# Loads, global keys and output products rescheduled in a fused attention and feed-forward kernel

## The chip, the cores and the metric

The kernel runs on one core of a Trainium2 chip. The metric is the device time of one execution in microseconds (us). Several executions are taken of each kernel, and the kernel before is run on the same chip in the same rounds. Medians and ranges are of all runs; where a slow run moves a median, the median of the fast runs stands beside it.

## The reference, cut to what matters

Attention with four batches, eight heads, 768 positions and 64 features; a query sees the first 8 keys (the global keys) and the last 96. A SwiGLU feed-forward block follows, on the 3072 tokens that come out.

```python
scores = scale * np.matmul(q, k.transpose(0, 1, 3, 2))
is_global = pos[None, :] < 8
is_local = (rel >= 0) & (rel < 96)
dist = np.where(is_global & ~is_local, 96.0, np.abs(rel))
scores = np.where(is_global | is_local, scores - slopes * dist, -1e9)
a = softmax(scores)                     # written out in the reference
x = (a @ v).transpose(0, 2, 1, 3).reshape(3072, 512)
g = x @ w_gate                          # 512 -> 1536
out = (g * sigmoid(g) * (x @ w_val)) @ w_out
```

## The kernel before

TensorE works on fp16 operands. The feed-forward part goes in eight tiles of 384 tokens, each with twelve groups of hidden features: a gate product (`gps`), a value product (`vps`), then the sum-times-gate product (`sl`) and the hidden row (`hT`) on VectorE. The output product of a tile is cut into parts of three matmuls, which are spread over the next tile. The attention of batch (block) b feeds tiles 2b and 2b+1, and its steps are put between the feature groups of the tiles before.

Keys go in seven chunks of 120. A chunk fills 128 rows: eight global rows, then 120 keys of its own. Block 0 is done in two halves of 384 queries, so that the feed-forward part can start early. Chunk 3 holds keys 360 to 479. Half 0 ends at query 383, so of chunk 3 its queries see only the first 24 keys:

```python
SCORES = {(0, 0): [(0, 0, 0, 216), (1, 216, 120, 216)],
          (0, 1): [(2, 0, 240, 144), (3, 144, 360, 24)],   # (chunk, column, first query, queries)
          ...

def load_v_rest(b, c):
    n = min(KC, S - KC * c)                                # KC = 120
    nc.gpsimd.dma_start(
        out=vSs[b][NG:NG + n, c, :, :],                    # NG = 8
        in_=v[b, :, KC * c:KC * c + n, :].rearrange("h p d -> p h d"))
```

The products of weights and values are these. `side is None` gives the denominators, a side gives the numerators:

```python
def weigh(self, half, dst, side):
    parts = self.parts(half)
    for i, (c, cb, col, o, n) in enumerate(parts):
        vals = vSs[b][:, c]
        for j in range(4):
            r = slice(32 * j, 32 * j + 32)
            nc.tensor.matmul(
                dst[r, o:o + n],
                lhsT=ones[:, 0:32] if side is None else vals[:, 4 * g + j, side::2],
                rhs=pairs[b, 2 * g + j // 2].at[cb][:, j % 2, col:col + n],
                start=(i == 0), stop=(i == len(parts) - 1), ...)
```

Heads go in pairs. Block 0 and pairs 0 and 1 of block 1 are transposed by TensorE. Pairs 2 and 3 of block 1 and all of blocks 2 and 3 are loaded as rows (`kst`, `qst`) and transposed by a DMA that SyncE issues. Their eight global rows of each chunk are cleared, and GpSimd copies the global keys in after the transpose:

```python
def stage(b):
    ...
    nc.gpsimd.memset(kend[b], 0.0)
    nc.gpsimd.memset(kst[b][0:NG, 768 * (0 if b > 1 else 2):], 0.0)

def global_keys(self):                                     # of a pair, after its DMA transpose
    k3 = self.kT.rearrange("r (c m) -> r c m", m=128)
    first = k3[:, 0, NG:2 * NG]
    nc.gpsimd.tensor_copy(
        out=k3[:, 0:J, 0:NG], in_=first.unsqueeze(1).broadcast_to([128, J, NG]))
    nc.gpsimd.tensor_copy(out=kE[:, self.hp, 0:NG], in_=first)
```

All loads are issued by GpSimd, in program order. The whole early list is:

```python
for c in range(4):
    load_v_rest(0, c)
...                                  # head: fillers, first transposes
load_w(0, 4); load_w(4, 6)           # gate and value weights of feature groups
load_half(1, 0, H)                   # k and q of block 0, half 1
load_w(6, 8); load_w(8, 10)
for c in range(4, NCH):
    load_v_rest(0, c)
load_w(10, 12)
stage(1); load_qk(1)
for g in range(3):
    load_wo(g)                       # output weights
load_globals()
...                                  # v chunks 0-3, ends, rows of pairs 2 and 3, v chunks 4-6 of block 1
```

The softmax here doesn't subtract the row's maximum and nothing guards it: scores larger than these inputs give would overflow.

## Time and profile before

| what | before |
|---|---|
| median time of the first three runs (range) | 256.95 us (254.27 to 257.81) |
| span of the profiled run, mean granted TensorE clock | 253.7 us, 0.991 |
| TensorE busy | 95% of the span |
| first feature group of tile 0 starts | 16.84 us |
| scores of pair 3 of block 1 start | 68.94 us |
| first gate of tile 2 starts | 78.55 us |

The page gives busy shares by engine and by fortieths of the span. The list of waits tells what ended TensorE's idle time, and the timeline places each of these waits. A timeline row gives the start and the length in us, the engine, the line of the kernel, the operation with output and inputs, the shapes and how many instructions the row merges. A number in brackets at its end is the idle time before the row, with what ended it. The lines are shown in the prediction.

### The profile page before, as it was taken

To read this page: it belongs to the slowest core of one execution; us is meant where nothing else is said; L and a number is where in the kernel's file an instruction comes from. 1 tells how busy PE (TensorE), PEld (TensorE's weight loads), DVE (VectorE), ACT (ScalarE), POOL (GpSimd) and SP (SyncE) were. 2 spreads that over 40 slices of the span, in tenths; PEclk is the share of its full clock that TensorE was granted. 3 is DMA by queue.
4 is the path that set the end of the run, shared out by engine and by line. 5 is a ranking of instruction groups with operands and counts; after the bars stand their busy time and mean duration, and the time that the engine had idled before them with its cause. 6 is when DMAs were issued, how large, how long until landed. Compare 5 with 4: busy or idle time off the path is not lost.

```text
span 253.7 us, 6001 instructions
## 1 busy us (share of the span) xinstructions
PE 240.2 (95%) x2380; PEld 135.3 (53%) x2380; DVE 157.5 (62%) x338; ACT 129.6 (51%) x288; POOL 127.5 (50%) x161
## 2 busy tenths in 40 slices
PE   7998998989799999979999999999999999999994
PEld 4554665545355555544555555555555555555543
DVE  4477766557575666772775666776775567555510
ACT  4746677785453744543563564455734643332321
POOL 8965996392319998918808877813020232300000
PEclk9999999999999999997999999999999999999999
DMA  8999999999911999999933999991011101101122
GB/s 153 164 193 193 171 145 194 177 131 123 145 41 44 89 143 125 170 150 98 110 55 25 125 133 179 151 122 45 0 44 41 41 3 45 41 3 41 41 83 83
DMA packets 93251, 25.76 MB, mean 102 GB/s; under 512 B 81480, under 2 KB 90280, under 8 KB 93224
## 3 DMA queue, kind: packets, MB, share of 16 engines
q0 software_dynamic: 71088, 14.00, 73.4%
q1 hardware_dynamic: 21576, 11.03, 22.6%
q8 instruction: 18, 0.29, 0.5%
q10 hardware_dynamic: 560, 0.36, 0.4%
q14 instruction: 9, 0.07, 0.1%
HBM read 28.58 MB, written 6.29 MB: 137 GB/s over the span
## 4 chain that ended last, share of the span: by engine, by line
PE 73%; DMA 14%; ACT 4%; POOL 3%; DVE 2%; issue 1%; DVEq 0%; POOLq 0%
PE ops L537 22%; PE gps L508 21%; PE vps L508 21%; DMA vS<-in_v_dram 5%; DMA q<-in_q_dram 4%; PE sc L364 3%; DMA qT<-qst 3%; PE num L435 3%; DMA wv<-in_moe_w_val_dram 3%; PE den L435 2%; POOL vS L160 1%; ACT at L372 1%; ACT th L519 1%; PE ops L553 1%; PE sc L328 1%
## 5 line engine op out<-in xcount | busy, mean ns | idle before, releaser
L521 DVE SCALAR_TENSOR_TENSOR sl<-th,gps 128x384 f32<-128x384 f32 x94 | 52.0, 553 | 57.2 <-ACT th L519 56.5
L519 ACT ACTIVATE th<-gps 128x384 f32<-128x384 f32 x94 | 46.6, 496 | 64.3 <-PE gps L508 62.7
L508 PE MATMUL gps<-xT,wg 128*128 128x384 f16 x376 | 77.5, 328 | 1.6 <-DVE xT L470 1.5
L508 PE MATMUL vps<-xT,wv 128*128 128x384 f16 x376 | 77.3, 328 | 1.5 <-DVE sl L521 1.5
L537 PE MATMUL ops<-wo,hT 128*128 128x512 f16 x276 | 73.6, 382 | 0.0
L525 DVE TENSOR_TENSOR hT<-vps,sl 128x384 f16<-128x384 f32 x94 | 51.9, 552 | 9.1 <-PE vps L508 2.2
L508 PEld LDWEIGHTS <-wg 128*128 128x128 f16 x384 | 36.6, 98 | 34.6 <-issue 3.7
L508 PEld LDWEIGHTS <-wv 128*128 128x128 f16 x384 | 36.6, 98 | 27.4 <-issue 3.7
L470 POOL TENSOR_TENSOR xT<-ns,rb 128x384 f16<-128x384 f32 x24 | 24.0, 1017 | 46.4 <-DVE rb L451 45.3
L372 ACT ACTIVATE at<-sc 128x432 f16<-128x432 f32 x72 | 33.3, 534 | 11.5 <-PE sc L364 11.5
L537 PEld LDWEIGHTS <-hT 128*128 128x128 f16 x276 | 26.1, 98 | 24.1 <-issue 1.5
L160 POOL DMA_DIRECT2D vS<-in_v_dram x28 | 24.9, 899 | 1.1 <-issue 1.0
L543 ACT ACTIVATE osb<-ops 128x512 f32<-128x512 f32 x23 | 13.7, 597 | 18.5 <-PE ops L537 18.5
L184 POOL DMA_DIRECT2D kst<-in_k_dram x20 | 17.7, 899 | 4.3 <-DMA wo<-in_moe_w_out_dram 4.3
L466 ACT COPY ns<-num 128x384 f32<-128x384 f32 x28 | 12.0, 482 | 12.7 <-PE num L435 12.7
L184 POOL DMA_DIRECT2D qst<-in_q_dram x20 | 17.2, 879 | 0.1
L383 DVE TENSOR_TENSOR at<-at,masks 128x864 f16<-128x864 f16 x20 | 12.4, 620 | 7.6 <-ACT at L372 7.6
L435 PE MATMUL num<-at,vS 128*32 128x216 f16 (+6 forms) x576 | 12.5, 225 | 2.0 <-DMA vS<-in_v_dram 2.0
L383 POOL TENSOR_TENSOR at<-at,masks 128x864 f16<-128x864 f16 x4 | 7.3, 1818 | 13.3 <-ACT at L372 13.3
L347 ACT ACTIVATE at<-sc 128x432 f16<-128x432 f32 (+2 forms) x32 | 11.6, 455 | 2.6 <-PE sc L339 2.6
L435 PEld LDWEIGHTS <-vS 128*32 128x32 f16 x576 | 10.0, 95 | 2.5 <-DMA vS<-in_v_dram 2.5
L364 PE MATMUL sc<-qT,kT 64*128 64x216 f16 (+2 forms) x148 | 9.7, 249 | 1.4 <-DMA qT<-qst 1.4
(69 smaller groups left out, 175.0 us busy)
## 6 DMA issues: line engine op xcount, KB each, us to landing
out_dram<-osb SPq DMA_DIRECT2D x23, 256.0 KB, 2.8
vS<-in_v_dram POOLq DMA_DIRECT2D x24, 120.0 KB, 6.8
qst<-in_q_dram POOLq DMA_DIRECT2D x20, 96.0 KB, 5.3
kst<-in_k_dram POOLq DMA_DIRECT2D x20, 90.0 KB, 4.3
wo<-in_moe_w_out_dram POOLq DMA_DIRECT2D x3, 512.0 KB, 10.7
wg<-in_moe_w_gate_dram POOLq DMA_DIRECT2D x8, 128.0 KB, 7.8
wv<-in_moe_w_val_dram POOLq DMA_DIRECT2D x8, 128.0 KB, 7.7
wg<-in_moe_w_gate_dram POOLq DMA_DIRECT2D x2, 256.0 KB, 6.6
```

What stands on the lines that cost most here:

```text
L160: nc.gpsimd.dma_start(out=vSs[b][NG:NG + n, c, :, :], in_=v[b, :, KC * c:KC * c + n, :].rearrange("h p d -> p h d"))
L184: nc.gpsimd.dma_start(out=rows_of(st, b, h // 2)[p0:p0 + n, :, h % 2, :], in_=src[b, h, 0:n * J].rearrange("(t p) d -> p t d", p=n))
L364: nc.tensor.matmul(sc[hi][:, col:col + n], lhsT=keys, rhs=self.qT[r, q0:q0 + n], start=True, stop=True)
L372: nc.scalar.activation(out=at[:, hi, :], in_=sc[hi][:, 0:BANK], func=AF.Exp, scale=scale)
L383: mul_eng.tensor_mul(at, at, m[:, :, o:o + BANK])
L435: nc.tensor.matmul(dst[r, o:o + n], lhsT=ones[:, 0:32] if side is None else vals[:, 4 * g + j, side::2], rhs=pairs[b, 2 * g + j // 2].at[c ...
L470: mul_eng.tensor_mul(self.x_out(half, side), srcs[side], self.rb)
L508: nc.tensor.matmul(gv[f, which][:, 0:TB], lhsT=w[:, c, 128 * f:128 * f + 128], rhs=x_of(t)[:, c, :], start=(c == 0), stop=(c == NC - 1))
L519: nc.scalar.activation(out=th, in_=dst[:, 0:TB], func=AF.Tanh, scale=0.5)
L521: nc.vector.scalar_tensor_tensor(out=sl, in0=th, scalar=1.0, in1=dst[:, 0:TB], op0=AluOp.add, op1=AluOp.mult)
L525: nc.vector.tensor_mul(hTs[t][:, f, :], dst[:, 0:TB], gv["sl"])
L537: nc.tensor.matmul(ops, lhsT=hTs[t][:, f, 128 * i:128 * i + 128], rhs=wo[:, f, :], start=(f == 0), stop=(f == NFF - 1))
```

## The change

It is one schedule change with several parts:

- Global keys of all blocks are loaded once (`kG`), and DMAs on SyncE's queue copy them into the rows before the transpose. So the clearing and the copies on GpSimd go.
- Block 1's loads are reordered. The output weights come ahead of the q and k rows, and pair 2 comes ahead of v.
- The last feature group of tile 0 carries four output parts, so these lie between half 1 and block 1. Tile 1 carries two parts in three groups. (In the lists of stretches below, the last two numbers of an entry shift when its attention steps come: work that is kept free of steps at the end, and a head start of the first step.)
- A group's masks (exponentials on ScalarE) are issued after its tanh instead of ahead of it.
- In the head, the first transposes and scores are reordered, there are three more fillers, and one weight load is split.
- The copies of v's global rows are issued two feature groups earlier.
- Of v chunk 3 of block 0, the 24 rows that half 0 needs are loaded early. The other 96 come after the weights of groups 8 and 9.

```diff
 def stage(b):
-        nc.gpsimd.memset(kst[b][0:NG, 768 * (0 if b > 1 else 2):], 0.0)
+        nc.sync.dma_start(out=kend[b][0:NG], in_=kG[:, b])
+        for hp in by_dma(b):
+            pair = kG[:, b, 2 * hp:2 * hp + 2, :].rearrange("p h d -> p (h d)")
+            nc.sync.dma_start(
+                out=rows_of(kst, b, hp)[0:NG].rearrange("p t e d -> p t (e d)"),
+                in_=pair.unsqueeze(1).broadcast_to([NG, J, 2 * D]))
...
-    def load_v_rest(b, c):
-        n = min(KC, S - KC * c)
+    def load_v_rest(b, c, r0=0, r1=KC):
+        r1 = min(r1, S - KC * c)
         nc.gpsimd.dma_start(
-            out=vSs[b][NG:NG + n, c, :, :],
-            in_=v[b, :, KC * c:KC * c + n, :].rearrange("h p d -> p h d"))
+            out=vSs[b][NG + r0:NG + r1, c, :, :],
+            in_=v[b, :, KC * c + r0:KC * c + r1, :].rearrange("h p d -> p h d"))
...  (global_keys and its calls go; load_globals loads kG too)
-    for c in range(4):
+    cut = TB - 3 * KC
+    for c in range(3):
         load_v_rest(0, c)
+    load_v_rest(0, 3, 0, cut)
...  (head: fill(14) -> fill(17), order of transposes and scores)
-    load_w(0, 4)
+    load_w(0, 2)
+    load_w(2, 4)
     load_w(4, 6)
     load_half(1, 0, H)
     load_w(6, 8)
     load_w(8, 10)
+    load_v_rest(0, 3, cut, KC)
     for c in range(4, NCH):
         load_v_rest(0, c)
     load_w(10, 12)
-    stage(1)
-    load_qk(1)
     for g in range(3):
         load_wo(g)
     load_globals()
+    stage(1)
+    load_qk(1)
...  (then ends, pair 2, v chunks 0-3, pair 3, v chunks 4-6)
-        (ff(0, 4, 12), half1, 1.0),
-        (ff(1, 0, 3) + ff(1, 3, 12, (1, 1, 2)), first(1), 6.0),
+        (ff(0, 4, 11) + [(0, 11, 4)], half1, 5.4, 0.4),
+        (ff(1, 0, 12, (0, 1, 1)), first(1), 6.0, -0.1),
...  (masks go to after_gate, run when a group's tanh is issued)
```

More of the change, by code (lines that the diff above doesn't have):

```diff
@@ L156, in load_qk @@
                 out=whole(st, b), in_=src[b, 0:NP].rearrange("h (p j) d -> p h (j d)", p=128))
-    def load_v_rest(b, c):
-        n = min(KC, S - KC * c)
+    def load_v_rest(b, c, r0=0, r1=KC):
+        r1 = min(r1, S - KC * c)
         nc.gpsimd.dma_start(
-            out=vSs[b][NG:NG + n, c, :, :],
-            in_=v[b, :, KC * c:KC * c + n, :].rearrange("h p d -> p h d"))
+            out=vSs[b][NG + r0:NG + r1, c, :, :],
+            in_=v[b, :, KC * c + r0:KC * c + r1, :].rearrange("h p d -> p h d"))
     vG = sb.tile([NG, B, H, D], FP16, name="vG")
+    kG = sb.tile([NG, B, H, D], FP16, name="kG")
     def load_globals():
-        nc.gpsimd.dma_start(
-            out=vG[:, 1:].rearrange("p b h d -> p (b h) d"),
-            in_=v[1:, :, 0:NG, :].rearrange("b h p d -> p (b h) d"))
+        for dst, src in ((kG, k), (vG, v)):
+            nc.gpsimd.dma_start(
+                out=dst[:, 1:].rearrange("p b h d -> p (b h) d"),
+                in_=src[1:, :, 0:NG, :].rearrange("b h p d -> p (b h) d"))
     def copy_globals(b):
@@ L398, in transposes_dma @@
                     in_=rows_of(st, b, hp).rearrange("p t e d -> p (t e d)"))
-        def global_keys(self):
-            k3 = self.kT.rearrange("r (c m) -> r c m", m=128)
-            first = k3[:, 0, NG:2 * NG]
-            nc.gpsimd.tensor_copy(
-                out=k3[:, 0:J, 0:NG], in_=first.unsqueeze(1).broadcast_to([128, J, NG]))
-            nc.gpsimd.tensor_copy(out=kE[:, self.hp, 0:NG], in_=first)
     class Quad:
@@ L586 @@
     V, A = nc.vector.tensor_copy, nc.scalar.copy
-    fill(14)
+    fill(17)
     A(out=q16[:, 0, 0:2], in_=q32)
@@ L609, with load_pair @@
     load_globals()
+    stage(1)
+    load_qk(1)
+    def load_pair(b, hp):
+        for i in (1, 0):
+            for e in range(2):
+                load_rows(b, i, 2 * hp + e)
+    load_ends(1)
+    load_pair(1, 2)
     for c in range(4):
         load_v_rest(1, c)
-    load_ends(1)
-    for hp in by_dma(1):
-        for i in (1, 0):
-            for e in range(2):
-                load_rows(1, i, 2 * hp + e)
+    load_pair(1, 3)
     for c in range(4, NCH):
@@ L619 @@
     p_bias(0, 0, "a0", "a1")
-    sc00 = pairs[0, 0].sc
-    p_bias(0, 1, "a2", "a3")
-    pairs[0, 0].scores_half(0, 0, sc00)
-    p_sc(0, 1)
     p_tr(1, "x2", "o0", V)
+    p_sc(0, 0)
+    p_sc(0, 1, "a2", "a3")
     p_bias(1, 0, "x0", "x1")
-    p_tr(2, "a0", "a1", A)
+    p_tr(2, "a0", "a1", V)
     p_sc(1, 0)
@@ L632 @@
     p_sc(2, 1, "a2", "a3")
+    p_sc(3, 0, "a0", "a1")
     for side, tag in enumerate(("x1", "x2")):
         quads[0, 0].numerators(side, single("num", tag))
-    p_sc(3, 0, "a0", "a1")
     p_sc(3, 1, "a2", "a3")
@@ L682, in fetch @@
         return step
-    def gk(b, *hps):
-        return lambda: [pairs[b, hp].global_keys() for hp in hps]
     def first(b):
         return [[tr(b, 0), tr(b, 1), fetch(b, 2, 3)], [sc(b, 0, 0), sc(b, 0, 1)],
-                [sc(b, 1, 0), sc(b, 1, 1), gk(b, 2)], [va(b, 0, 0), gk(b, 3)],
+                [sc(b, 1, 0), sc(b, 1, 1)], [va(b, 0, 0)],
                 [sc(b, 2, 0), sc(b, 2, 1)], [sc(b, 3, 0), sc(b, 3, 1)], [va(b, 1, 0)]]
@@ L696, in both @@
         return [[sc(b, 0, 2), sc(b, 1, 2)], [sc(b, 2, 2), sc(b, 3, 2), fetch(n, 0, 1)],
-                [va(b, 0, 1)], [va(b, 1, 1), gk(n, 0, 1)],
+                [va(b, 0, 1)], [va(b, 1, 1)],
                 [sc(n, 0, 0), sc(n, 0, 1), fetch(n, 2, 3)], [sc(n, 1, 0), sc(n, 1, 1)],
-                [va(n, 0, 0), gk(n, 2, 3)], [sc(n, 2, 0), sc(n, 2, 1)],
+                [va(n, 0, 0)], [sc(n, 2, 0), sc(n, 2, 1)],
                 [sc(n, 3, 0), sc(n, 3, 1)], [va(n, 1, 0)]]
@@ L710 @@
     stretches = [
-        (ff(0, 0, 4), [], 0),
-        (ff(0, 4, 12), half1, 1.0),
-        (ff(1, 0, 3) + ff(1, 3, 12, (1, 1, 2)), first(1), 6.0),
-        (ff(2, 0, 12, (1,)) + ff(3, 0, 12, (1,)), both(1), 6.0),
-        (ff(4, 0, 12, (1,)) + ff(5, 0, 12, (1,)), both(2), 6.0),
-        (ff(6, 0, 12, (1,)), second(3), 6.0),
-        (ff(7, 0, 12, (1,)), [], 0)]
-    loads = {}
+        (ff(0, 0, 4), [], 0, 0),
+        (ff(0, 4, 11) + [(0, 11, 4)], half1, 5.4, 0.4),
+        (ff(1, 0, 12, (0, 1, 1)), first(1), 6.0, -0.1),
+        (ff(2, 0, 12, (1,)) + ff(3, 0, 12, (1,)), both(1), 6.0, 0.4),
+        (ff(4, 0, 12, (1,)) + ff(5, 0, 12, (1,)), both(2), 6.0, 0.4),
+        (ff(6, 0, 12, (1,)), second(3), 6.0, 0.4),
+        (ff(7, 0, 12, (1,)), [], 0, 0)]
+    loads, after_gate = {}, {}
     def at_step(t, f, *fns):
@@ L724 @@
     for h in range(H):
-        at_step(h // 4, 1 + h % 4, lambda h=h: make_masks(h, WIN, 3 * WIN))
-        at_step(h // 4, (8, 1)[h // 4] + h % 4, lambda h=h: make_masks(h, 0, WIN))
-    at_step(1, 0, lambda: [copy_globals(b) for b in range(1, B)])
+        for (t, f), c0, c1 in zip((((0, h), (0, 8 + h)), ((1, h - 4), (1, h - 2)))[h // 4],
+                                  (WIN, 0), (3 * WIN, WIN)):
+            after_gate.setdefault((t, f), []).append(
+                lambda h=h, c0=c0, c1=c1: make_masks(h, c0, c1))
+    at_step(0, 10, lambda: [copy_globals(b) for b in range(1, B)])
     for b, base, rate, v_at in ((2, 24, 2.0, (30, 31, 32, 32, 37, 38, 39)), (3, 43, 1.4, (54, 55, 56, 57, 61, 62, 63))):
@@ L741 @@
     outs = [(t, i, part) for t in range(NT - 1) for i in range(3) for part in range(4)]
-    for tiles, steps, tail in stretches:
+    for tiles, steps, tail, owed in stretches:
         groups = []
@@ L748 @@
         quota = len(steps) / (work - tail)
-        owed = 0.4
         for w, t, f, which in groups:
@@ L760 @@
                 gate_or_val(t, f, which, NC if t == 0 and f < 2 else 0)
+                for fn in after_gate.pop((t, f), []):
+                    fn()
             owed += w * quota
@@ L767 @@
         assert not steps
-    assert not later and not loads and not outs
+    assert not later and not loads and not after_gate and not outs
     for i in range(2):
```

## The prediction

> **What bounds the kernel now.** I read the page first (busy time and slices), then TensorE's waits, then TensorE's timeline around each wait, then the timelines of GpSimd and SyncE to see what released it.
>
> ```profile
> PE 240.2 (95%) x2380; PEld 135.3 (53%) x2380; DVE 157.5 (62%) x338; ACT 129.6 (51%) x288; POOL 127.5 (50%) x161
> PE   7998998989799999979999999999999999999994
> DMA  8999999999911999999933999991011101101122
> ```
>
> TensorE bounds it: 95% busy, no other engine above 62%. From the nineteenth slice (about 120 us) on, every slice is full until the last; its timeline from 119.6 us has no idle time marked before the closing products. So time can only be won before 120 us, and only what TensorE stands still or runs slow. The DMA engines are full in slices 1 to 11 (to about 70 us) and 14 to 21 (82 to 120 us): in both stretches a transfer cannot come sooner without another coming later.
>
> ```profile
> PE num L435 <- DMA vS<-in_v_dram: 2.0, 3, 1.0
> PE vps L508 <- DVE sl L521: 1.5, 2, 1.0
> PE gps L508 <- DVE xT L470: 1.5, 1, 1.5
> PE sc L364 <- DMA qT<-qst: 1.4, 1, 1.4
> PE den L435 <- DVE at L380: 0.5, 1, 0.5
> ```
>
> Columns: total us, times, longest. These are few and single waits, so each can be placed in the timeline:
>
> ```profile
> 44.87 0.79 PE L508 MATMUL gps<-xT,wg 128*128 128x384 f16 x2 [1.47 <-DVE xT L470]
> 52.24 0.81 PE L508 MATMUL vps<-xT,wv 128*128 128x384 f16 x4 [1.02 <-DVE sl L521]
> 65.76 0.55 PE L364 MATMUL sc<-qT,kT 64*128 64x216 f16 x8 [1.39 <-DMA qT<-qst]
> 114.50 0.25 PE L435 MATMUL num<-at,vS 128*32 128x144 f16 x4 [1.00 <-DMA vS<-in_v_dram]
> 115.97 1.40 PE L508 MATMUL gps<-xT,wg 128*128 128x384 f16 x4
> 119.60 0.81 PE L508 MATMUL gps<-xT,wg 128*128 128x384 f16 x4
> ```
>
> Starts of consecutive gate and value groups stand 0.65 us apart when nothing waits (237.00 after 236.35 us); that is my unit below, and three output products also take 0.65. Measured against it, the standing times are: 1.95 us at 43 to 45.5 (wait and the slow pair after it), 1.2 at 51, 0.6 at 59.6, 1.55 at 64, 0.9 at 72, and 2.5 at 112 to 115. The row at 115.97 takes 1.40 where the same one at 119.60 takes 0.81: the clock was halved after that wait, from 115.97 to 119.6, which costs another 1.55 us. Together 10.3 us, plus about 2 us in the first 26.
>
> GpSimd's timeline shows why the loads come when they do:
>
> ```profile
> 33.62 0.76 POOL L155 DMA_DIRECT2D kst<-in_k_dram  x1
> 43.84 0.61 POOL L190 DMA_DIRECT2D kend<-in_k_dram  x1 [2.18 <-DMA wo<-in_moe_w_out_dram]
> 46.87 0.84 POOL L184 DMA_DIRECT2D kst<-in_k_dram  x1 [2.42 <-DMA wo<-in_moe_w_out_dram]
> 49.59 0.84 POOL L184 DMA_DIRECT2D kst<-in_k_dram  x1 [1.88 <-DMA wo<-in_moe_w_out_dram]
> 78.93 2.65 POOL L148 MEMSET kst<- 8x3072 f16 x1
> 81.53 1.76 POOL L184 DMA_DIRECT2D kst<-in_k_dram  x2
> 108.71 0.22 POOL L403 COPY kT<-kT 128x48 f16<-128x48 f16 x1 [1.39 <-DMA kT<-kst]
> ```
>
> The three output weights land about 2.9 us apart (issues released at 43.84, 46.87, 49.59). Block 2's loads start at 81.53, after a 2.65 us clearing of eight rows. Global-key copies hold GpSimd until a transpose has landed.
>
> [...]
>
> **The change part by part.**
>
> *Output products between half 1 and block 1.* Four output parts, 4 x 0.65 = 2.6 us, now stand between the last value group of tile 0 and the first gate of tile 1, where TensorE stood 1.95 us for the normalised rows. Enough to cover it: gain 1.95. Tile 1 keeps eight instead of twelve parts, so no work is added.
>
> *Head.* Deferring 96 of 120 rows of one v chunk (chunks land about 0.9 us apart) brings half 1's q that much sooner. TensorE waited for it at 25.6 us, so about 0.9 us is gained. The reordered transposes, the three extra fillers and the split weight load can start the gates sooner, but the q transfer then catches TensorE again; I count no more.
>
> *Loads of block 1 reordered: the price.* The whole-row k and q loads now stand behind the output weights. They landed at 38.4 and 40.4 us (issues 33.62 and 34.37, 4.8 and 6.1 us to landing); three output weights of 2.9 us and two small loads put q at 40.4 + 8.9 + 0.6 = 49.9. Its transposes on TensorE started at 46.90 before. Now they come after five units from the first gate of tile 1, which starts at 42.91 + 2.6 - 0.9 = 44.6: at 47.8. k is just there, q not, so a new wait of about 1.7 us. Leaving the transposes at 51.0, TensorE has done six units (3.9 us) more than before at 48.36: the net gain so far is 3.9 - 2.65 = 1.25, of 2.85.
>
> *Masks follow the tanh.* Removes two exponentials (0.88 us) ahead of a tanh at 50.3. With an output part before the scores as well, the 1.2 us at 51 should go: +1.2.
>
> *Pair 2 before v.* Its loads come four v chunks sooner (4 x 0.9 us), so the 1.55 us wait for its qT goes: +1.55. That makes 4.0 at the scores of pair 3, at 68.94 + 1.3 - 4.0 = 66.2 (two output parts more are done by then). But pair 3 is still near the end of the same full DMA stretch. SyncE issued its last transpose at 62.77 to 64.9 us, and one takes 6.7 us (median) to land. I expect it at 66 to 68, so a wait of about 1.0 us there: 3.0 left.
>
> *No clearing, no key copies on GpSimd.* Per block 2.65 us of clearing and about 0.4 us per pair go. But the loads also stand behind the multiply for the last quad of block 1, and that quad now ends later relative to tile 2 (five units before its first gate, not seven). Loads started 3.0 us after that gate (78.55 to 81.53); I now get about 1.5. With the DMAs full throughout, v then lands 1.5 us sooner relative to TensorE: of 2.5 us wait about 1.2 stays, too little to halve the clock (at 43 us a similar wait did not). Gain 1.3 + 1.55 = 2.8.
>
> Sum: 3.0 + 2.8, plus 0.2 for the small wait at 72 us: 6.0. After 120 us I expect nothing: full before, full after. 256.95 - 6.0 = 250.9.
>
> **The rivals.** (1) *The DMAs are the bound to 68 us and take the early gain back.* They move the same bytes; if pair 3's last transpose lands at 69, [...] the first part gives 1 instead of 3, and the time is near 253. For it: full DMA slices, and transposes taking 5.6 and 6.7 us in company. Against: before, transposes and loads overlapped only late; now they overlap sooner. (2) *All waits vanish.* If whole-row q lands by 48 and v by 112, the gain is 1.95 + 0.9 + 1.2 + 1.55 + 4.0 = 9.6: 247.4. For it: the schedule's offset in block 1 was set to start the transposes one part later, as if fitted to that landing. (3) *SyncE becomes the wait.* The new copies stand in its queue ahead of transposes and stores, and wait for GpSimd to clear the end rows. Against: block 2's transposes started only at 87 us, 8 us after the clearing, so a copy has time; the stores are not on the path. If wrong, 1 to 3 us in each block: 253 to 256. (4) *The masks come too late* for block 1's multiply: unlikely, since they are still issued in tile 1's first gates.
>
> **Range and chances.** Runs of the kernel before spread over 3.5 us, and the gain is 6 give or take about 2. Eight times in ten: 248.0 to 253.6. The 2% line lies at 251.8, only 0.9 from my figure: faster 0.62, within 2% 0.37, slower 0.01.
>
> **What would show it.** Right: no wait for the normalised rows near 45 us; a wait for the q loads (one to two us) before block 1's transposes near 48; no wait of a value group on the sum-times-gate product at 51; no wait for pair 2's qT, perhaps one for pair 3's; the v wait before 115 us at half or less, with the clock full there; clearing of eight rows and key copies absent from GpSimd, block 2's loads starting about 1.5 us after tile 2's first gate. Wrong: a new wait over 2 us for a transpose or a transfer from the global keys, or a halved clock near 50 us; or, the other way, none at 48 us.

## The result, and the profile after

The changed kernel takes 265.42 us (median of 4 runs, 264.77 to 267.25); the kernel before, on the same chip, takes 256.63 (254.27 to 257.81). The ratio is 1.037, with a 95% interval of 1.028 to 1.046: slower by 3.7%. Here and below a ratio is the mean time of one kernel's fast runs over the mean of the other's of the same rounds, so it is not quite the ratio of the medians. The prediction had the sign wrong, and the time lies far outside its range.

The slices show at once where. This is the page of the changed kernel (span 263.6 us, so a slice is 6.6 us): TensorE's busy tenths, then its granted clock.

```profile
PE   7900298999989999999999999999999999999995
PEclk9975569999999999999999999999999999999999
```

TensorE does nothing in the third and fourth slice (13 to 26 us), and the clock is low from the third to the sixth. Away from this hole it is nearly full. The list of TensorE's waits names it, and next to it all else is small (total us, times, longest):

```profile
PE num L435 <- DMA vS<-in_v_dram: 18.1, 1, 18.1
PE vps L508 <- DVE sl L521: 1.1, 2, 0.6
```

One single wait of 18.1 us is twice the whole loss. The timeline of TensorE places it in the numerators of half 0:

```profile
13.05 0.43 PE L435 MATMUL num<-at,vS 128*32 128x216 f16 x12 [0.16 <-DMA vS<-vG]
31.54 0.72 PE L435 MATMUL num<-at,vS 128*32 128x24 f16 x20 [18.05 <-DMA vS<-in_v_dram]
...
34.75 0.82 PE L508 MATMUL gvps<-xT,wg 128*128 128x384 f16 x2
...
37.24 0.49 PE L508 MATMUL gvps<-xT,wg 128*128 128x384 f16 x2
```

The same place in the kernel before, also in the timeline of TensorE:

```profile
13.21 0.72 PE L435 MATMUL num<-at,vS 128*32 128x216 f16 x32
...
16.84 0.34 PE L508 MATMUL gvps<-xT,wg 128*128 128x384 f16 x1
```

The shapes tell which products these are. Twelve matmuls of chunks 0, 1 and 2 go through; then the row starts with the form `128x24`: 128 rows of contraction and 24 queries. That is chunk 3, the only part with 24 queries. It contracts over 128 rows, not over 8 + 24 = 32. Before, all 32 matmuls of the two sides went through in one row. GpSimd's timeline in the changed kernel shows the two loads, and the chain that ended last shows the transfer as one of its pieces:

```profile
4.39 3.38 POOL L165 DMA_DIRECT2D vS<-in_v_dram  x4
...
26.01 3.27 POOL L165 DMA_DIRECT2D vS<-in_v_dram  x4
```

```profile
26.01 5.48 DMA vS<-in_v_dram
31.54 0.72 PE num L435 x16
```

The row at 4.39 has the first three chunks and the 24 rows of the fourth. The row at 26.01 begins with the 96 deferred rows, which stand behind twenty weight loads and half 1's k and q. They land at 31.49 us, and the products start 0.05 us later. TensorE waits for rows that are multiplied by weights that the mask made zero: in this program the matmul over 128 partitions waits for all 128, needed or not.

The clock has its part. In the tables of stretches (length, then busy us and instructions of PE, PEld, DVE, ACT and POOL, then granted clock, DMA share and GB/s; the share adds up the packets' times, so it can pass 1) the changed kernel has

```profile
13.00:31.00 18.00, 0.43 (x12) 0.24 (x12) 0.13 (x1) 0.88 (x2) 15.40 (x21) 0.60 1.55 182
31.00:38.00 7.00, 6.46 (x89) 4.09 (x90) 3.49 (x7) 0.75 (x3) 6.97 (x11) 0.56 1.28 152
```

where the kernel before has

```profile
13.00:31.00 18.00, 16.56 (x223) 9.80 (x221) 13.94 (x35) 9.91 (x26) 12.74 (x18) 1.00 1.51 188
```

After the wait TensorE works at about half speed until 37.2 us: the pair of matmuls at 34.75 takes 0.82, the same pair at 37.24 takes 0.49. The DMA engines are as busy in both kernels (1.55 and 1.51, 182 and 188 GB/s): while TensorE stands, the loads run on. The delay shrinks on the way:

| start of, us | before | after | after minus before |
|---|---|---|---|
| first feature group of tile 0 | 16.84 | 34.75 | 17.9 |
| scores of pair 3 of block 1 | 68.94 | 84.65 | 15.7 |
| first gate of tile 2 | 78.55 | 92.38 | 13.8 |
| end of the span | 253.7 | 263.6 | 9.9 |

The 1.5 us for the normalised rows, the 1.4 us for pair 2's qT, and the waits for v with the slow clock after them (112 to 120 us in the kernel before) no longer appear. This profile alone can't say whether the change removed them or the 18 us by which the loads are now ahead of TensorE. What the change itself is worth has to be found without the stall; runs 1 and 2 tell the two apart, and the end of "Why the prediction was wrong" does the sum.

### The profile page after: what moved, and what is told of

The parts are those of the page before. It is cut to its first block, busy times and chain, and to the rows that moved or that the text cites.

```text
span 263.6 us, 5995 instructions
## 1 busy us (share of the span) xinstructions
PE 239.0 (91%) x2383; PEld 135.3 (51%) x2383; DVE 157.1 (60%) x339; ACT 129.5 (49%) x287; POOL 120.3 (46%) x144
## 2 busy tenths in 40 slices
DMA packets 95362, 25.93 MB, mean 98 GB/s; under 512 B 82544, under 2 KB 92392, under 8 KB 95336
## 4 chain that ended last, share of the span: by engine, by line
PE 70%; DMA 10%; POOL 9%; ACT 5%; DVE 4%; issue 2%; POOLq 0%; DVEq 0%
PE ops L537 20%; PE vps L508 19%; PE gps L508 19%; DMA vS<-in_v_dram 7%; PE num L435 3%; DMA q<-in_q_dram 3%; PE sc L371 2%; PE den L435 2%; POOL wv L216 2%; POOL vS L165 2%; ACT at L379 2%; POOL wg L216 2%; DVE sl L521 1%; ACT th L519 1%; POOL xT L470 1%
## 5 line engine op out<-in xcount | busy, mean ns | idle before, releaser
L435 PE MATMUL num<-at,vS 128*32 128x216 f16 (+6 forms) x576 | 13.1, 233 | 18.4 <-DMA vS<-in_v_dram 18.1
L491 DVE TENSOR_TENSOR xT<-num,rb 128x384 f16<-128x384 f32 x4 | 2.1, 554 | 18.8 <-PE num L435 18.7
```

What stands on the lines that cost most here:

```text
L435: nc.tensor.matmul(dst[r, o:o + n], lhsT=ones[:, 0:32] if side is None else vals[:, 4 * g + j, side::2], rhs=pairs[b, 2 * g + j // 2].at[c ...
```

## The experiments

Theory D (deferred rows): the loss is the numerators' wait for the 96 rows, and nothing else in the change costs. Rival L: the loss lies in the other new DMAs, the copies of global keys and the reordered loads, and the wait on v is only where it shows. Rival C: chunk 3 is late anyway because the early DMAs are full, so the deferral only names the wait. The later runs ask what the rest of the change is worth, part by part. Each run is correct against the reference. "The base" below is the changed kernel with chunk 3 loaded whole, the first run.

### 1. Chunk 3 whole and early

```diff
-    cut = TB - 3 * KC
-    for c in range(3):
+    for c in range(4):
         load_v_rest(0, c)
-    load_v_rest(0, 3, 0, cut)
...
-    load_v_rest(0, 3, cut, KC)
```

> The changed kernel with v chunk 3 of block 0 loaded whole and early again; all other parts kept. Theory A (the 18 us wait for the 96 deferred rows is the whole loss, and the rest of the change gains about what was predicted): no wait of the first numerators beyond 0.5 us, clock full by 10 us, time 250 to 252.5. Rival B (another part of the change costs too, such as the new copies on SyncE or the reordered loads, and is hidden behind the long wait): 255 or more, with a new wait of over 2 us after 40 us.

Measured: 251.52 us (249.75 to 253.04), before 255.32 in the same rounds; ratio 0.986 (0.978 to 0.993). The 14 us are gone with the one load put back. The numerators run in one row again, and the gates of tile 0 start at 15.30 us, earlier than in the kernel before. The list of waits and rows from the timeline of TensorE:

```profile
PE trs L299 <- DMA q<-in_q_dram: 2.0, 2, 1.9
...
PE sc L371 <- DMA qT<-qst: 0.7, 1, 0.7
```

```profile
12.82 0.72 PE L435 MATMUL num<-at,vS 128*32 128x216 f16 x32
...
25.81 0.36 PE L299 MATMUL trs<-ident,q 128*64 128x128 f16 x6 [1.86 <-DMA q<-in_q_dram]
...
26.54 1.46 PE L508 MATMUL gps<-xT,wg 128*128 128x384 f16 x4
...
68.81 0.55 PE L371 MATMUL sc<-qT,kT 64*128 64x216 f16 x8 [0.68 <-DMA qT<-qst]
```

So rival C falls, and so does L as a cause of the loss: the copies and the new order are all still there. What TensorE gains in the head it waits for q of half 1 at 25.8 us, and the clock is halved after that (1.46 us for a group of 0.81), from 26.25 to 29.67 us by the trace's clock records. The profiled execution of this run is the fastest of its four (249.75 us), so where profiles are compared with it below, the base looks up to 1.8 us better than its median.

### 2. The deferral alone, in the kernel before

```diff
-    for c in range(4):
+    for c in range(3):
         load_v_rest(0, c)
+    load_v_rest(0, 3, 0, cut)
...
     load_w(8, 10)
+    load_v_rest(0, 3, cut, KC)
```

> The kernel before with only the deferral: chunk 3 in two parts, the 96 rows behind the half-1 loads. Theory A: the same wait of 15 to 18 us at the first numerators, about 2 us of half clock after it, less the waits for transfers that it absorbs (0.5, 1.5, perhaps 4): 268 to 275. Rival B (the deferral costs only in company of the other parts): within 2 us of the kernel before.

Measured: 271.67 us (270.99 to 272.40); ratio 1.065 (1.058 to 1.072). From its timeline of TensorE:

```profile
30.21 0.72 PE L435 MATMUL num<-at,vS 128*32 128x24 f16 x20 [18.05 <-DMA vS<-in_v_dram]
```

The same row with the same wait, to a hundredth. The deferral makes the loss by itself; without the rest of the change it is even larger by 6 us. The other waits of the kernel before are mostly still there: 1.5 us for the normalised rows, 1.7 for the sum-times-gate product and another 1.8 for v, with a halved clock at 131.5 us. Only the 1.4 us for qT is gone.

### 3. The deferral kept, half 0 contracts over the 32 rows that it needs

```diff
                 vals = vSs[b][:, c]
+                kr = 32 if (b == 0 and half == 0 and c == 3) else 128
...
-                        lhsT=ones[:, 0:32] if side is None else vals[:, 4 * g + j, side::2],
-                        rhs=pairs[b, 2 * g + j // 2].at[cb][:, j % 2, col:col + n],
+                        lhsT=ones[0:kr, 0:32] if side is None else vals[0:kr, 4 * g + j, side::2],
+                        rhs=pairs[b, 2 * g + j // 2].at[cb][0:kr, j % 2, col:col + n],
```

> The changed kernel, deferral kept, but the products of chunk 3 in half 0 contract over the 32 rows that hold keys of that half instead of all 128 rows. Theory A: those products then read none of the deferred rows, so the wait goes although the rows still land at 31 us; time as with the whole chunk or up to 1 us less, 249 to 252.5. Rival (the wait came from the queue's order or from the late landing of something else): the wait stays, 263 to 267.

Measured: 254.51 us (253.31 to 255.88); ratio 0.998 (0.991 to 1.005). The rows land as late as in the changed kernel (issued at 26.95 us, landed at 32.11), and the long wait is gone all the same, as TensorE's timeline and GpSimd's show:

```profile
12.96 1.04 PE L436 MATMUL num<-at,vS 128*32 128x216 f16 x32
...
26.95 3.28 POOL L165 DMA_DIRECT2D vS<-in_v_dram  x4
```

This separates "the rows are late" from "the products read rows that they don't need", and it is the second. But this kernel is slower than the base by about 3 us, where I had expected the deferral, once freed, to be worth something. The 32-row products are no faster (1.04 us for the row, 0.72 in the base), so the gates of tile 0 start 1 us later (16.29 us); but q of half 1 lands only at 25.93, and TensorE waits for it in both kernels. In its timeline new waits stand further back:

```profile
69.86 0.55 PE L371 MATMUL sc<-qT,kT 64*128 64x216 f16 x8 [3.66 <-DMA qT<-qst]
```

That is pair 2, whose q transpose SyncE issued at 58.75 us; and the third output weight is waited for (1.75 us) at 46.99 us.

### 4. The 96 rows sooner, after the weights of four groups

```diff
     load_w(2, 4)
+    load_v_rest(0, 3, cut, KC)
     load_w(4, 6)
...
-    load_v_rest(0, 3, cut, KC)
```

> The changed kernel with the 96 rows placed behind the weights of the first four feature groups instead of behind those of ten. They land at about 18.3 us instead of 31.5. Theory A: the wait shrinks to about 5 us and ends where they land; half clock follows; time 252 to 257. Rival (a fixed cost): unchanged at 265.

Measured: 252.51 us (251.53 to 253.09); ratio 0.989 (0.981 to 0.996).

```profile
18.08 0.72 PE L435 MATMUL num<-at,vS 128*32 128x24 f16 x20 [4.54 <-DMA vS<-in_v_dram]
```

The end of the wait moves with the load: 31.54 to 18.08 us. That settles theory D. What is left is a wait of 4.54 us and a halved clock until 23.4 us. By the medians it costs about 1 us against the base, within the spread, and by the profiles 3.3 (span 251.3 against 248.0). The profiles show where part of it is taken back: the gates of tile 0 start 6.0 us after those of the base (21.30 against 15.30), but the first value group after half 1's transposes only 3.1 after (32.48 against 29.36), because the base stands there for q and then runs at half clock.

### 5. Block 1's loads in their old order (on the base)

```diff
-    for g in range(3):
-        load_wo(g)
     load_globals()
     stage(1)
     load_qk(1)
+    for g in range(3):
+        load_wo(g)
...  (then v chunks 0-3, ends, pairs 2 and 3, v chunks 4-6, as before)
```

> The mended kernel (v chunk 3 whole and early, 251.5 us) with block 1's loads in the order of before: whole rows ahead of the output weights, v ahead of pair 2. Theory (the prediction's price and gain): no wait before block 1's transposes, but the output products ahead of tile 1 now wait for the third output weight, which lands near 49 us instead of 45: a wait of 3 to 4 us there, and pair 2's qT wait back. Time 253 to 257. Rival (the order gains nothing, since the same bytes move): within 1 us of the mended kernel.

Measured: 257.36 us (256.41 to 260.39; 256.59 without the slow run), before 254.57 (253.42 without its slow runs); ratio 1.011 (1.002 to 1.020). From the list of waits:

```profile
PE ops L537 <- DMA wo<-in_moe_w_out_dram: 6.6, 3, 3.3
```

The four output parts ahead of tile 1 need all three output weights, which land too late in the old order: waits of 3.34, 2.56 and 0.71 us from 43.8 us on, where 3 to 4 were expected, and the clock is halved from 48.6 to 58.9 us. Pair 2's qT wait, which was expected back, is not in the list. So the moved output products can't do without the moved loads. No run undoes both together, so what the two are worth as one part is not shown.

### 6. Output parts back in tile 1 (on the base)

```diff
-        (ff(0, 4, 11) + [(0, 11, 4)], half1, 5.4, 0.4),
-        (ff(1, 0, 12, (0, 1, 1)), first(1), 6.0, -0.1),
+        (ff(0, 4, 12), half1, 1.0, 0.4),
+        (ff(1, 0, 3) + ff(1, 3, 12, (1, 1, 2)), first(1), 6.0, 0.4),
```

> The mended kernel with the output parts back in tile 1 and block 1's first step where it was. Theory: the wait for the normalised rows (1.95 us) is back and a new one for the whole q rows appears before block 1's transposes (1 to 3 us): 253 to 257. Rival (the moved products only shift a wait, because the DMAs bound the stretch to 68 us): within 1 us of the mended kernel, with the qT wait near 68 us shorter by what the others grew.

Measured: 251.06 us (250.67 to 253.63); ratio 0.990 (0.981 to 0.999). Within the spread the same as the base (0.986). TensorE's timeline shows the wait for the normalised rows back, as it should be, and two more at block 1's transposes:

```profile
44.55 0.79 PE L508 MATMUL gps<-xT,wg 128*128 128x384 f16 x2 [1.47 <-DVE xT L470]
...
47.58 0.53 PE L271 MATMUL trs<-ident,kst 128*64 128x128 f16 x12 [0.94 <-DMA kst<-in_k_dram]
...
49.50 0.53 PE L271 MATMUL trs<-ident,qst 128*64 128x128 f16 x12 [1.39 <-DMA qst<-in_q_dram]
```

The three waits sum to 3.8 us. At the scores of pair 3 no wait is left: they start at 68.33 us, but with two output parts (1.3 us) fewer done than in the base, which comes there at 68.13 and stands until 68.81. Tile 2's first gate starts at 77.93 us against 76.52 in the base, and the span ends at 248.9 against 248.0. So the moved output parts are worth between nothing (the medians) and 1.4 us (the profiles), not the 3.8 us of waits that they remove. The comparison is not clean: in this profile the clock stays full, in that of the base it is halved after 25.8 us, and at half 1's last numerators run 6 is already 2.05 us ahead (41.23 us against 43.28). It gives this back by the output parts and the waits that follow.

### 7. Clearing and key copies back on GpSimd (on the base)

```diff
-        nc.sync.dma_start(out=kend[b][0:NG], in_=kG[:, b])
...  (the copies into the pairs' rows)
+        nc.gpsimd.memset(kst[b][0:NG, 768 * (0 if b > 1 else 2):], 0.0)
...  (global_keys and its calls come back; kG goes)
```

> The mended kernel with the clearing and the key copies back on GpSimd, no global-key copies on SyncE. Theory (the prediction's 2.8 us): block 2's loads start about 3 us later, the v wait near 111 us grows from 0.5 to 2 to 3 us, perhaps with half clock: 253 to 256. Rival (the copies on SyncE cost as much as they save): within 1 us of the mended kernel or faster.

Measured: 253.92 us (252.77 to 255.70); ratio 1.000 (0.991 to 1.008), against 0.986 for the base: 1.4% of 254.6 us is 3.5 us. GpSimd's timeline with the clearing:

```profile
79.53 2.65 POOL L148 MEMSET kst<- 8x3072 f16 x1
82.13 1.75 POOL L185 DMA_DIRECT2D kst<-in_k_dram  x2
```

and that of the base, where the load starts without it:

```profile
77.67 1.74 POOL L191 DMA_DIRECT2D kst<-in_k_dram  x2
```

The waits for v come back in part (1.6 us in two, against 0.3 in the base), and so does a wait of 1.8 us for qT. Of the parts undone one at a time, this is the only one whose undoing costs time without stalling another part; in the same rounds runs 6 and 8 take 251.06 and 250.36 us. With the intervals of both ratios the 3.5 us may be anything from about 0.6 to 6.4. Counted from tile 2's first gate (78.38 us here, 76.52 in the base) block 2's loads start 3.75 us after it here and 1.15 in the base: the difference is the clearing. But 1.9 of the 4.3 us between the two profiles are lost ahead of that gate, where the wait for qT stands, and 2.4 after it.

### 8. Masks ahead of the tanh again (on the base)

```diff
-            after_gate.setdefault((t, f), []).append(
-                lambda h=h, c0=c0, c1=c1: make_masks(h, c0, c1))
+        at_step(h // 4, 1 + h % 4, lambda h=h: make_masks(h, WIN, 3 * WIN))
+        at_step(h // 4, (8, 1)[h // 4] + h % 4, lambda h=h: make_masks(h, 0, WIN))
```

> The mended kernel with the masks ahead of the tanh. Theory (the prediction's 1.2 us): a wait of a value group for the gate's product of about 1 us more near 56 us; but the DMAs end their burst near 68.8 us anyway and a qT wait stands there, so only part shows: 251 to 253. Rival: faster than the mended kernel, because a later tanh costs nothing and masks come sooner.

Measured: 250.36 us (249.76 to 251.05); ratio 0.986 (0.978 to 0.994), the same as the base. The waits for the sum-times-gate product are 1.5 us in three against 1.1 us in two. So the order of the masks is worth 0.4 us in the waits and nothing in the time. This profile also has a shorter wait for q of half 1 (1.1 us, not 1.9) and no halved clock after it, some 2.4 us less lost early than in run 1, and yet tile 2's first gate starts at 76.29 us against 76.52: 1.4 us of waits for qT stand in between instead of 0.7, and 0.6 us for an output weight is new.

### 9. The head's part alone, in the kernel before

```diff
-    fill(14)
+    fill(17)
...
-    load_w(0, 4)
+    load_w(0, 2)
+    load_w(2, 4)
...  (order of the first transposes and scores as in the change)
```

> The kernel before with only the head of the change: transposes reordered, 17 fillers, first weight load in two parts; v chunk 3 whole. Theory (the head's gain is taken back by half 1's q, which lands near 25.5 us in every run): the first gates start 1 to 1.5 us sooner, the wait at half 1's q transposes grows by as much, time within 1 us of the kernel before. Rival (the full clock from 6 us carries through): 1.5 to 2.5 us faster than before.

Measured: 257.06 us (256.66 to 259.12), before 256.17; ratio 1.012 (1.000 to 1.024). The gates start at 15.38 us instead of 16.84, and then, from TensorE's timeline:

```profile
25.28 0.36 PE L292 MATMUL trs<-ident,q 128*64 128x128 f16 x6 [1.53 <-DMA q<-in_q_dram]
```

Of the 1.46 us won, 1.17 are waited for at once (a wait of 1.53 us, where the kernel before has 0.36). The head brings nothing by itself, as the prediction said of it. The fast runs are even slower by 1.2%, at the edge of the interval; theory expected at most 1 us, and no run says why.

### 10 and 11. The tail of v later; and half 1's first step later too (on the base)

Two tries to beat the base. Run 10 issues v chunks 4 to 6 of block 1 in tile 1 instead of ahead. Run 11 starts half 1 later as well, so that q of half 1 has landed.

```diff
-    for c in range(4, NCH):
-        load_v_rest(1, c)
...
+    for c in range(4, NCH):
+        at_step(1, 8, lambda c=c: load_v_rest(1, c))
```

```diff
-        (ff(0, 0, 4), [], 0, 0),
-        (ff(0, 4, 11) + [(0, 11, 4)], half1, 5.4, 0.4),
+        (ff(0, 0, 5), [], 0, 0),
+        (ff(0, 5, 11) + [(0, 11, 4)], half1, 5.4, -0.2),
```

> The mended kernel with the last three v chunks of block 1 issued in tile 1's ninth feature group, when the DMA burst is over, instead of inside it. Theory (the full DMAs, not TensorE, set when pair 3's scores can start near 69 us): its last transpose lands 1 to 3 us sooner, the qT wait near 68 us goes, time 0.5 to 2 us below the mended kernel: 249 to 251. Rival (the transposes' own latency sets it): the wait stays, within 0.5 us of 251.5.

Measured: 251.56 us (249.70 to 254.90; 250.94 without the slow run), before 256.17 (255.03 without its slow runs); ratio 0.986 (0.974 to 0.998). Its profiled run is the slow one of the four, so nothing is read from that profile, and whether the wait for qT goes in a fast run is not shown. The ratio is that of the base: no gain in the time.

> The run before with half 1's first step two groups later, so that TensorE has work while half 1's q is on its way. Theory: the 2 us wait at 24 us falls under 0.7 and the clock stays full there (1.7 us of half clock went with it in the mended kernel's profile), 1 to 3 us more gained, if pair 3's transpose is in time: 247 to 250. Rival (the DMA burst to 68 us takes it all back): as the run without it, with a qT wait of 2 to 3 us near 67 us.

Measured: 249.98 us (249.63 to 253.22), before 256.17; ratio 0.985 (0.973 to 0.997). The wait for q falls from 1.9 to 1.1 us and not under 0.7, the wait for qT is gone, and 0.8 us for a gate weight is new. The clock, expected full, is halved all the same, from 27.9 to 31.3 us.

### 12, 13 and 14. Runs 3, 1 and 11 again, five rounds each on one chip

> Same kernel as e3. If the deferral has a cost of its own (weights of the output product landing 1 to 2 us later, and with them everything behind), it stays 1.5 to 3.5 us above e13. If e3 was a bad draw, within 1 us of e13.

> Same kernel as e1, beside the other two in the same rounds: 250.5 to 252.5 us, ratio to the kernel before 0.980 to 0.990.

> Same kernel as e11: if holding half 1 back gains at all, 0.5 to 2 us below e13; if the DMAs take it back, within 0.5 us of e13.

Measured beside 255.61 us for the kernel before (254.53 without its two slow runs):

| kernel | median us (range) | ratio (95%) |
|---|---|---|
| 32 rows, deferral kept | 253.61 (251.51 to 254.55) | 0.994 (0.989 to 1.000) |
| chunk 3 whole (the base) | 251.51 (250.39 to 256.69; 250.72 without the slow run) | 0.987 (0.981 to 0.994) |
| base, v tail and half 1 later | 251.35 (248.51 to 252.04) | 0.985 (0.978 to 0.991) |

Both of the lower two beat both kernels, by 1.3 to 1.6% against the one before and about 5% against the changed one (251.5 over 265.4, medians of different rounds). They are not to be told apart, as the expectation had it for the case that the DMAs take the gain back, and neither reaches 2%. In two sets of rounds the freed deferral is 2 to 3 us slower than the whole load. Its intervals overlap a little with those of the base, so this is likely rather than proven. In both of its profiles the third output weight lands some 2 us later (46.95 and 47.25 us against 44.93 and 44.86). Part of this is the issuing: the split load is one DMA more, GpSimd takes 3.28 us for four v loads where the base takes 2.50 for three, and the output weights are issued 0.9 and 1.6 us later (33.20 against 32.28, 33.55 against 31.98). The rest is left open.

## Why the prediction was wrong

**The step that failed.** It is in the part on the head: "Deferring 96 of 120 rows of one v chunk (chunks land about 0.9 us apart) brings half 1's q that much sooner. ... so about 0.9 us is gained." The deferral was treated as a transfer moved in a queue, with a gain for what stands behind it. Nobody asked who reads the rows, and whether the reader comes before the new landing. It came 18 us before it. In place of +0.9 stands a wait of 18.05 us and half speed until 37.2 us, which left 8.8 us beyond the kernel before and 13.9 beyond run 1. Run 2 makes the wait alone, run 1 removes it alone, run 3 removes it with the rows still late, and run 4 moves it with the load. Even the 0.9 is not found: q of half 1 landed at 25.01 us in the changed kernel and at 25.53 in the kernel before, but with the deferral freed at 25.93 and 26.27 (runs 3 and 12), against 25.76 and 25.42 with chunk 3 whole (runs 1 and 13).

The failure could have been seen before any run of the change. `weigh` slices neither operand by rows, and the trace of the kernel before shows the 16 numerators of chunk 3 in half 0 with the form `128*32 128x24` (tile `vS`, between 13.2 and 16.7 us): all 128 rows, the 96 among them. In the changed kernel the products that waited began 0.05 us after the transfer's landing (31.54 and 31.49 us). Among four rivals none was about a reader that the change left behind; the copies on SyncE, which worried me, did no harm that a run shows.

**The rest, term by term.** Without the deferral the sum of the prediction is 6.0 - 0.9 = 5.1 us. Run 1 measured (1 - 0.9856) x 255.3 = 3.7 us and run 13 (1 - 0.9871) x 255.6 = 3.3. The base, at 251.5 us, would have been inside the range. But the right total hides terms that were wrong:

- *Output products, 1.95.* The wait for the normalised rows went, as said. In time it is between 0 and 1.4 us (run 6, with a clock that differs): the median with the wait put back is no longer.
- *Price of the reordered loads, a wait of 1.7 at 47.8.* In the base it is not there, as its transposes start only at 50.61 us. TensorE had stood earlier, for q of half 1 at 25.8 us (1.86) and at half speed for 3.4 us after it. In run 6, where TensorE comes sooner, it is there with 0.94 for k and 1.39 for q. The landing was right (q at 49.00 us in the base and 49.46 in run 6, 49.9 predicted); TensorE's arrival in the base was not.
- *Masks, 1.2.* Nothing in the time (run 8).
- *Pair 2, 1.55, with 1.0 left at pair 3.* The base has no wait for pair 2 and 0.68 for pair 3. TensorE comes to pair 3's scores at 68.13 us, where I expected 66.2, and starts them at 68.81; the kernel before has 68.94.
- *Clearing and copies, 2.8.* Between tile 2's first gate and the end the base gains 3.7 us (2.0 ahead at 76.52 against 78.55, and 5.7 ahead at the end, 248.0 against 253.7). Run 7's profile puts 2.4 of that to this part, near the 2.8. It also puts 1.9 us ahead of tile 2, where the prediction gave this part nothing; in the ratios both together are 3.5. The block's loads start 1.15 us after the gate (1.5 predicted; 77.67 - 76.52). The wait for v before it is 0.3, where I left 1.2.

One reading of the prediction is a little off, and nothing rests on it: the full DMA slices after the gap are 14 to 20 (82 to 127 us), not 14 to 21 (82 to 120).

The first rival, that the DMAs take part of the early gain back, fits the runs in its mechanism: pair 3 starts near 69 us as it said, not near 67. Tile 2's first gate starts at 76.52, 76.29, 76.53, 76.64 and 76.56 us in runs 1, 8, 11, 13 and 14, although these lose different amounts before 32 us: what one saves early it waits for later, for qT, for a weight or for q. In size it lies halfway: that stretch was to bring 3.0 us, or 1.0 under the rival, and the base has 2.0.

**What the 18 us wait cost.** Set beside run 1 and not the kernel before, the changed kernel is 19.5 us late at tile 0's first group, 15.8 at pair 3's scores (84.65 and 68.81), 15.9 at tile 2's first gate (92.38 and 76.52) and 15.6 at the end. (The medians say 13.9, as run 1's profile is a fast one.) So some 3.6 us are taken back, before pair 3's scores, where run 1 stands for q at half 1 and for qT and runs at half clock. After that nothing is. Run 2 says the same: with the same wait in the kernel before, the profile is 16.3 us late at tile 2's first gate (94.89 and 78.55) and 16.5 at the end. The rest of what the table above shows as made up, 0.5 us by tile 2's first gate and 3.7 after it, is the gain of the change itself, which run 1 has too. So here the wait cost less than its length only by what TensorE would later have waited for transfers that ran on meanwhile.

## What to carry to other kernels

When a load is split or put off, list its readers first, by what each of them addresses and not by what its result needs: here the products waited 18.05 us for 96 rows that were masked to zero (the changed kernel and run 2), and no longer once their operand was cut to 32 rows (run 3). If a part of a tile is to come late, cut the readers to the rows that are there, and then still measure, as here loading the tile whole was as good or better (251.51 us against 253.61, runs 13 and 12). Where transfers set the pace of a stretch, look for a wait that is removed on the compute engine at the next transfer: here tile 2's first gate started between 76.29 and 76.64 us in five runs that lost different amounts before 32 us. So price such gains at the end of the stretch and not wait by wait.

## What else the traces measured

- *The clock after short waits.* In run 1 a wait of 1.86 us for q of half 1 was followed by a halved clock for 3.4 us (26.25 to 29.67 us; a group took 1.46 us). In run 9 a wait of 1.53 us at the same place was not: the next group took 0.82 us. What decides between the two is not shown.
- *DMA transposes beside other loads.* In the kernel before the median from issue to landing is 5.6 us (k) and 6.7 us (q), and in run 3 a q transpose issued at 58.75 us held its reader until 69.86.
- *Clearing by GpSimd, in the kernel before.* 8 x 3072 elements took 2.65 us, 8 x 1536 took 1.37 and 128 x 512 took 0.51 to 0.54: the first has a sixteenth of the rows of the last and six times the row length, and took five times as long.
